# First expert layer with the hidden units on the partitions: w1 blocks as the stationary operand, 128 token slots moving

## The chip, the cores and the metric

The kernel runs on one core of one Trainium2 chip. The metric is the device time of a run in microseconds. The trace is one profiled run of the same program; its span is about 2 us shorter than the time. In the lines of the profile PE is TensorE, PEld its weight loads, PEldq the sequencer that feeds both, DVE is VectorE, ACT ScalarE, POOL GpSimd and SP SyncE. Runs over 1.5% above the fastest of the same kernel are called slow and are left out of comparisons.

## The reference, cut to what matters

The first half is a linear attention (8 batches, 8 heads, 576 positions). Its output `x` (4608 tokens of 512) goes through a mixture of 8 experts:

```python
h = np.maximum(x[b, s] @ w1[e], 0.0)          # 512 -> 1024
out[b, s] = p[e] * (h @ w2[e])                # 1024 -> 512
```

The expert `e` of a token is known only at run time: the argmax of a gate, or, behind a second gate, the expert of the token before.

## The kernel before

The kernel sorts tokens into pages of 128 slots, all of one expert. There are 38 pages here, in two epochs. The number `ev` (expert times the columns of one expert) is loaded into a TensorE register for each page, and every matmul that needs w1 or w2 addresses it through that register. Both weights lie complete in SBUF in bf16. This is the first layer of a page, with its transposes, and the second layer:

```python
def hidden(n, xt, ev_src, mid=lambda: None):
    ev = nc.values_load(ev_src, engines=(PE,), ...)
    h_ps = ps_p.tile([128, 8, 128], F32, name="pj").rearrange(...)
    for c in range(2):
        for dc in range(DC):                   # DC = 4
            nc.tensor.matmul(h_ps[:, c, :], lhsT=xt[:, dc, :],
                             rhs=w1_all[:, ds(ev + (dc * F + c * 512), 512)],
                             start=(dc == 0), stop=(dc == DC - 1))
        if c == 0:
            mid()                              # turns the next page's x
    h = arena[:, n % 3].rearrange("p (f c) -> p f c", c=128)
    nc.scalar.activation(h, h_ps..., Act.Relu)
    return h, ev

def hidden_t(h, n=FC):                         # FC = 8
    tp = ps_t.tile([128, FC, 128], BF, name="tp")
    for f in range(n):
        nc.tensor.transpose(tp[:, f], h[:, f], ident_bf)
    ...
    nc.vector.tensor_copy(ht[:, 0:n], tp[:, 0:n])
    if n < FC:                                 # the other half by DMA
        nc.sync.dma_start_transpose(out=ht[:, n:], in_=h[:, n:]...)

# output(), the second layer
for f in range(FC):
    nc.tensor.matmul(y_ps[:, 0, :], lhsT=htn[0][:, f],
                     rhs=w2_all[:, ds(ev + f * D, D)], ...)
```

Pages 0 to 16 are computed up to the relu while w2 is still being loaded. From page 17 on, first layers alternate with outputs, three outputs for two pages.

The softmax here doesn't subtract the row's maximum and nothing guards it: scores larger than these inputs give would overflow.

Of the kernel before, what the change touches and what calls it, by code (L numbers as in the profile page):

```python
# [23 lines left out]
NEP = 18  # L24
# [6 lines left out]
def kernel(  # L31
# [296 lines left out]
    rmask = consts.tile([128, 2, 9], F32)  # L328
    ids2 = consts.tile([128, 18, 2], BF)
    wt8 = consts.tile([128, E], F32)  # L330
    io128 = consts.tile([128, 128], BF)
    cpg = consts.tile([128, NC], F32)
# [8 lines left out]
    def gate_consts():  # L341
        wg3 = consts.tile([128, 2, 4, E + 1], BF)
        wgr = consts.tile([128, 4, E + 1], F32)
        nc.gpsimd.tensor_tensor(ident2, ident[:, 0:64], ident[:, 64:128], op=Alu.add)
        nc.gpsimd.iota(io128, pattern=[[1, 128]], base=0, channel_multiplier=0, **fdt)
        yield
# [5 lines left out]
        for a in range(2):  # L352
# [3 lines left out]
        yield  # L356
        nc.gpsimd.iota(ids2[:, :, 0].rearrange("p (a r) -> p a r", a=2), pattern=[[128, 2], [0, 9]], base=0,
                       channel_multiplier=1, **fdt)
        nc.gpsimd.iota(ids2[:, :, 1].rearrange("p (a r) -> p a r", a=2), pattern=[[0, 2], [1, 9]], base=1,
                       channel_multiplier=0, **fdt)  # L360
        nc.gpsimd.iota(wt8, pattern=[[-1, E]], base=E, channel_multiplier=0, **fdt)
        nc.gpsimd.iota(cpg, pattern=[[1, NC]], base=0, channel_multiplier=0, **fdt)
        yield
        nc.gpsimd.memset(onesb, 1.0)
# [16 lines left out]

    def gate(ep, gt, n):


# [71 lines left out]
        nc.vector.tensor_scalar(gpg, code, scalar1=7, scalar2=None, op0=Alu.logical_shift_right)  # L456
        slf, col = t18("slf"), t18("col")
        nc.vector.tensor_copy(slf, slot)
        if ep == 0:
            nc.vector.tensor_copy(col, gpg)  # L460
        else:
            nc.vector.tensor_scalar(col, gpg, scalar1=float(NEP), scalar2=over, op0=Alu.is_ge, op1=Alu.mult)
            nc.vector.tensor_tensor(col, col, gpg, op=Alu.add)
        if ep:
            yield
            yield

        oh, pg = t18("oh", 128, BF), t18("pg", NC, BF)
        ri = gt.tile([128, n, 2, NC], BF, name="ri")

        def parts(r_, v_, t_):
            shape = list(r_.shape)
            nc.vector.tensor_tensor(r_, pg[:, t_].unsqueeze(2).to_broadcast(shape), v_[:, t_].unsqueeze(3).to_broadcast(shape),
                                    op=Alu.mult)

        def build(g):
            t_ = slice(n * g, n * g + n)
            nc.vector.tensor_tensor(oh[:, t_], io128.unsqueeze(1).to_broadcast([128, n, 128]),
                                    slf[:, t_].to_broadcast([128, n, 128]), op=Alu.is_equal)
            nc.vector.tensor_tensor(pg[:, t_], cpg.unsqueeze(1).to_broadcast([128, n, NC]),  # L480
                                    col[:, t_].to_broadcast([128, n, NC]), op=Alu.is_equal)
            parts(ri, ids2, t_)

        build(0)
        yield
        l_ps = ps_k.tile([128, 2, NC], F32, name="kv")
        for g in range(18 // n):
            for i in range(n):
                nc.tensor.matmul(l_ps.rearrange("p a c -> p (a c)"), lhsT=oh[:, n * g + i],
                                 rhs=ri[:, i].rearrange("p a c -> p (a c)"),  # L490
                                 start=(g == 0 and i == 0), stop=(n * g + i == 17))
            yield
            if n * (g + 1) < 18:
                build(g + 1)
                yield
# [33 lines left out]
        nc.vector.tensor_scalar(over, gbs[:, E:E + 1], scalar1=float(-NEP), scalar2=over, op0=Alu.add, op1=Alu.add)  # L529
        lists[ep] = dict(idr=idr, ix=ix, lid=lid, tmp=(ex, fr, m_, rs, oh, pg, parts))  # L530

    def both(ep, n):
        yield from gate(ep, gt, n)
        yield from probs(ep, gt)

    def probs(ep, gt):

        ex, fr, m_, rs, oh, pg, parts = lists[ep].pop("tmp")

# [3 lines left out]

        v3, pr = t18("v3", 3, BF), t18("pr")
        rp = gt.tile([128, 6, 3, NC], BF, name="rp")
        nc.vector.tensor_reduce(rs, ex, axis=AX, op=Alu.add)
# [4 lines left out]
        for i in range(2):  # L551
            nc.vector.tensor_copy(v3[:, :, i:i + 1], pr)
            nc.vector.tensor_tensor(v3[:, :, 2:3] if i else pr, pr, v3[:, :, i:i + 1], op=Alu.subtract)
        if ep:
# [3 lines left out]
        for g in range(3):  # L558
            parts(rp, v3, slice(6 * g, 6 * g + 6))
            yield  # L560
            for i in range(6):
                nc.tensor.matmul(p_ps.rearrange("p a c -> p (a c)"), lhsT=oh[:, 6 * g + i],
                                 rhs=rp[:, i].rearrange("p a c -> p (a c)"),
                                 start=(g == 0 and i == 0), stop=(g == 2 and i == 5))
            yield
# [37 lines left out]
    WH = 17  # L603
    outs, hs, done, spare = [], {}, [], list(range(3, 9))
    NST = 2 * NEP + 2

    def hidden(n, xt, ev_src, mid=lambda: None):
        ev = nc.values_load(ev_src, engines=(PE,), min_val=0, max_val=(E - 1) * WE,
                            skip_runtime_bounds_check_because="multiples of the columns of one expert")
        h_ps = ps_p.tile([128, 8, 128], F32, name="pj").rearrange("p (a x) c -> p a (x c)", a=2)  # L610
        for c in range(2):
            for dc in range(DC):
                nc.tensor.matmul(h_ps[:, c, :], lhsT=xt[:, dc, :], rhs=w1_all[:, ds(ev + (dc * F + c * 512), 512)],  # L613
                                 start=(dc == 0), stop=(dc == DC - 1))
            if c == 0:
                mid()
        h = arena[:, n % 3].rearrange("p (f c) -> p f c", c=128)
        nc.scalar.activation(h, h_ps.rearrange("p a x -> p (a x)").rearrange("p (c f) -> p f c", f=FC), Act.Relu)  # L618
        return h, ev

    def hidden_t(h, n=FC):

        tp = ps_t.tile([128, FC, 128], BF, name="tp")
        for f in range(n):
            nc.tensor.transpose(tp[:, f], h[:, f], ident_bf)  # L625
        n_ = spare.pop(0) if spare else 0
        ht = arena[:, n_].rearrange("p (f c) -> p f c", c=128) if n_ else moh.tile([128, FC, 128], BF, name="ht")
        nc.vector.tensor_copy(ht[:, 0:n], tp[:, 0:n])  # L628
        if n < FC:
            nc.sync.dma_start_transpose(out=ht[:, n:], in_=h[:, n:].rearrange("p f c -> p (f c)"))  # L630
        return ht, n_

    def output(pg, htn, ev, last=False):
# [3 lines left out]
        for f in range(FC):  # L637
            nc.tensor.matmul(y_ps[:, 0, :], lhsT=htn[0][:, f], rhs=w2_all[:, ds(ev + f * D, D)],  # L638
                             start=(f == 0), stop=(f == FC - 1))
        if htn[1]:  # L640
            spare.append(htn[1])
# [23 lines left out]
    def page(j, nw, gates):  # L665
# [8 lines left out]

        if j < NST:
            hs[j] = hidden(j, xts.pop(j), pages[j][1], mid)
        gate_part()
        if j >= 1:
            h, ev = hs.pop(j - 1)
            done.append((pages[j - 1], hidden_t(h, FC // 2 if NEP <= j < NST - 1 else FC), ev))  # L680
        gate_part()
# [25 lines left out]
    for P in range(NP):  # L707
        for g, i, d_ in LK:
            t = max(9 * P + d_, i - 2) if g == 0 else 9 * P + d_
            at(t, cast_k, P, g, i, 0 <= t < LAG - 4)  # L710
        for r in range(9):
            at(9 * P + LAG - 4 + r // 2, cast_q, P, r)
        if P + 1 < NP:
            if P:
                at(9 * P - 5, load, P + 1, "k", 0)
            at(9 * P + 5, load, P + 1, "v", 0)
            at(9 * P - 1, load, P + 1, "k", 1)
            at(9 * P + 9, load, P + 1, "v", 1)
            at(9 * P + LAG + 1, load, P + 1, "q", 0)
# [22 lines left out]
    for t in range(NK + LAG + 3):  # L742
# [45 lines left out]
        if tk:  # L788
            for _ in range(t > 8 and t % 5 in (0, 2, 4)):
                w_load()  # L790
        else:
            for _ in range(3 if 0 not in lists else 0):
                w_load()
        if t == NK + 1:

            kctx.close()
            w2_all = pool("w2p", 1, side="right", **rw).tile([128, E * WE], BF)
            wdst[1] = w2_all
            gt = pool("gt", 1, side="right", **rw)
            ga = both(0, 6)  # L800
            next(ga)
# [10 lines left out]
    mo2 = pool("mo2", 4, **rw)  # L812
    moh = pool("moh", WH - 5, **rw)
    ga = both(1, 6)
    next(ga)
    for j in range(early[0], NST + 1):
        page(j, 3, True)
# [12 lines left out]
    def rest(i):  # L830
        with tc.If(nov > i):
            for d in range(2):
                pg = pages[2 * NEP + i + d]
                h, ev = hidden(d, turn(fetch(pg[0])), pg[1])
                output(pg, hidden_t(h), ev)
            if i + 2 < NOV:
# [33 lines left out]
```

## Time and profile before

The median of three runs is 333.03 us (332.88 to 334.21), the profiled span 330.9 us.

| stretch of the span | what runs | PE busy of it | what sets its length |
|---|---|---|---|
| 0 to 126 us | attention | 70% (48 to 86% by 20 us) | mixed |
| 126 to 155 us | first routing | 11.7 of 29.0 us | a chain on DVE, DMA |
| 155 to 213.5 us | first layer of pages 0 to 16, second routing, w2 load | 49.9 of 58.5 us | mostly PE |
| 213.5 to 321 us | first layer of pages 17 to 37, all outputs | all of it | PE |

The prediction shows the lines.

### The profile page before, as it was taken

The numbers are of one execution on the slowest core, as the hardware profiler recorded it, in microseconds if no ns is written. First come the engines' busy times: TensorE is split into PE (matmuls) and PEld (weight loads), VectorE is DVE, ScalarE is ACT, GpSimd is POOL, SyncE is SP. The second block draws the span as 40 slices with busy tenths as digits, with TensorE's granted clock in tenths as the row PEclk, the third lists the DMA queues.
The fourth block names the chain that finished last, engine by engine and source line by source line (L and its number), as shares of the span: only waits on it lengthen the run. The fifth ranks groups of instructions, "written<-read, shape, count | busy, mean of one in ns | idle before, by whom it ended". The sixth has DMA issues, their size and how long they took to land. (4 is left out here: it accounts for less than half of the span.)

```text
span 330.9 us, 7843 instructions
## 1 busy us (share of the span) xinstructions
PE 257.2 (78%) x2789; PEld 151.7 (46%) x2809; DVE 183.2 (55%) x406; ACT 154.1 (47%) x230; POOL 195.8 (59%) x299
## 2 busy tenths in 40 slices
PE   2585488768787775722998885999999999999980
PEld 1464256546464553411565453554444444444430
DVE  2677188788879768980354776423333333323440
ACT  1586498888889865510555452532122221222000
POOL 3677787698498595356377653325555657432550
PEclk9859779999899959555799997999999999999996
DMA  7999989999888789999689996338668666532330
GB/s 230 391 411 408 315 238 326 368 271 301 285 239 259 239 150 202 224 223 222 130 167 206 226 226 164 81 82 184 171 173 176 189 148 171 168 112 79 129 133 32
DMA packets 52649, 69.89 MB, mean 211 GB/s; under 512 B 25552, under 2 KB 27088, under 8 KB 52608
## 3 DMA queue, kind: packets, MB, share of 16 engines
q0 software_dynamic: 14176, 31.14, 42.4%
q1 hardware_dynamic: 34352, 33.43, 30.9%
q10 hardware_dynamic: 4080, 4.77, 4.2%
q8 instruction: 26, 0.43, 0.5%
q14 instruction: 15, 0.12, 0.1%
HBM read 67.16 MB, written 14.68 MB: 247 GB/s over the span
## 5 line engine op out<-in xcount | busy, mean ns | idle before, releaser
L613 PE MATMUL pj<-w_all,xt 128*128 x291 | 75.2, 389 | 2.6 <-ACT xt L599 1.4
L618 ACT ACTIVATE arena<-pj 128x1024 bf16<-128x1024 f32 x38 | 38.9, 1023 | 75.3 <-PE pj L613 70.9
L644 POOL DMA_INDIRECT out_dram<-y,idr x38 | 37.8, 995 | 51.3 <-DVE y L643 47.3
L584 POOL DMA_INDIRECT xg<-x_tok,ix x36 | 37.4, 1038 | 27.3 <-PE tp L597 16.5
L212 DVE TENSOR_REDUCE kmx<-pj 128x8 f32<-128x1024 f32 x36 | 44.0, 1222 | 16.1 <-ACT kvb L251 8.4
L232 POOL TENSOR_TENSOR va<-vs,ek 128x512 bf16<-128x512 f32 (+1 forms) x40 | 38.2, 958 | 21.0 <-ACT ek L221 15.3
L156 POOL DMA_DIRECT2D w_all<-in_moe_w_dram x64 | 35.8, 565 | 16.4 <-DMA w_all<-in_moe_w_dram 15.3
L281 ACT ACTIVATE qp<-pj 128x1024 bf16<-128x1024 f32 x36 | 37.5, 1043 | 12.4 <-PE pj L275 12.3
L613 PEld LDWEIGHTS <-xt 128*128 128x128 bf16 x304 | 29.0, 99 | 30.2 <-issue 2.2
L218 ACT ACTIVATE kp<-pj 128x1024 bf16<-128x1024 f32 x36 | 37.3, 1037 | 11.2 <-DVE kmx L212 11.2
L643 DVE TENSOR_SCALAR y<-po,prb 128x512 f32<-128x512 f32 x24 | 18.0, 751 | 29.0 <-PE po L638 29.0
L183 PE MATMUL tp<-ident_bf,kb 128*128 128x128 bf16 x144 | 17.1, 246 | 17.1 <-POOL kb L110 8.1
L206 PE MATMUL pj<-om_bd,kt 128*128 128x256 bf16 x144 | 25.8, 310 | 2.9 <-ACT qp L281 1.8
L305 DVE TENSOR_TENSOR xr<-po,rd 128x512 bf16<-128x512 f32 x36 | 24.9, 692 | 1.2
L599 ACT COPY xt<-tp 128x512 bf16<-128x512 bf16 x18 | 10.5, 584 | 30.2 <-PE tp L597 29.1
L638 PE MATMUL po<-w_all,ht 128*128 x103 | 24.5, 379 | 0.1
L628 DVE COPY ht<-tp 128x1024 bf16<-128x1024 bf16 (+1 forms) x20 | 11.9, 597 | 22.5 <-PE tp L625 22.5
L116 POOL CAST qb<-arena 128x512 bf16<-128x512 f32 x36 | 21.1, 612 | 3.9 <-DMA arena<-in_q_dram 3.9
L729 ACT COPY qt<-tp 128x512 bf16<-128x512 bf16 x36 | 21.6, 601 | 3.6 <-DVE kt L727 2.7
L638 PEld LDWEIGHTS <-ht 128*128 128x128 bf16 x160 | 15.1, 98 | 16.1
L628 DVE COPY arena<-tp 128x512 bf16<-128x512 bf16 (+1 forms) x18 | 9.2, 514 | 22.0 <-PE tp L625 22.0
L727 DVE COPY kt<-tp 128x512 bf16<-128x512 bf16 x36 | 15.0, 417 | 11.3 <-PE tp L183 11.2
(152 smaller groups left out, 394.7 us busy)
## 6 DMA issues: line engine op xcount, KB each, us to landing
w_all<-in_moe_w_dram POOLq DMA_DIRECT2D x64, 256.0 KB, 7.9
vs<-in_v_dram SPq DMA_DIRECT2D x8, 1152.0 KB, 12.5
arena<-in_q_dram SPq DMA_DIRECT2D x4, 2304.0 KB, 15.1
ks<-in_k_dram SPq DMA_DIRECT2D x7, 1152.0 KB, 13.8
x_tok<-xr ACTq DMA_DIRECT2D x16, 256.0 KB, 5.7
ks<-in_k_dram SPq DMA_DIRECT2D x1, 640.0 KB, 5.6
out_dram<-y,idr POOLq DMA_INDIRECT x38, 2.9
xg<-x_tok,ix POOLq DMA_INDIRECT x36, 3.7
```

The source lines that it names most:

```text
L156: nc.gpsimd.dma_start(out=wdst[l][:, ds(e * WE + i * 1024, 1024)].rearrange("p (c f) -> p c f", f=w), in_=src[e].rearrange(("(c p) f -> p ...
L206: nc.tensor.matmul(pj[:, 2 * i:2 * i + 2, :].rearrange("p a d -> p (a d)"), lhsT=kts[t][:, i], rhs=om_bd, start=True, stop=True)
L212: nc.vector.tensor_reduce(mx, kpj[t], axis=AX, op=Alu.max)
L218: nc.scalar.activation(kp, kpj.pop(t), Act.Exp, scale=scale)
L232: nc.gpsimd.tensor_tensor(va[:, x, 0:Dh].rearrange("p (r h) d -> p r h d", h=4), vv, ek[:, x].rearrange("p (r h) o -> p r h o", h=4).to_br ...
L281: nc.scalar.activation(qp, qpj.pop(s), Act.Exp, scale=scale)
L305: nc.vector.tensor_tensor(xrs[s][:, u % 2, :].rearrange("p (g h d) -> p g h d", g=2, h=4), ov[:, :, :, 0:Dh], rd.to_broadcast([128, 2, 4, ...
L584: nc.gpsimd.indirect_dma_start(out=xg, out_offset=None, in_=src, in_offset=bass.IndirectOffsetOnAxis(ap=ix, axis=0), bounds_check=TE - 1, ...
L613: nc.tensor.matmul(h_ps[:, c, :], lhsT=xt[:, dc, :], rhs=w1_all[:, ds(ev + (dc * F + c * 512), 512)], start=(dc == 0), stop=(dc == DC - 1))
L618: nc.scalar.activation(h, h_ps.rearrange("p a x -> p (a x)").rearrange("p (c f) -> p f c", f=FC), Act.Relu)
L638: nc.tensor.matmul(y_ps[:, 0, :], lhsT=htn[0][:, f], rhs=w2_all[:, ds(ev + f * D, D)], start=(f == 0), stop=(f == FC - 1))
L644: s_ = nc.gpsimd.indirect_dma_start(out=out_flat, out_offset=bass.IndirectOffsetOnAxis(ap=idr[:, c:c + 1], axis=0), in_=y, in_offset=None, ...
```

## The change

A matmul has a stationary operand (`lhsT`, which a weight load fetches first) and a moving one (`rhs`). The new first layer makes 128 columns of w1 stationary and streams the 128 slots. The result comes out with units on the partitions, as the second layer wants its stationary operand, so neither transposes nor their copies are needed. Block `f` takes every eighth column, because w2 is stored with unit 8p+f on partition p.

```diff
-    def hidden(n, xt, ev_src, mid=lambda: None):
+    def hidden(xt, ev_src, mid=lambda: None):
...
-        for c in range(2):
+        h_ps = ps_p.tile([128, FC, 128], F32, name="pj")
+        for f in range(FC):
             for dc in range(DC):
-                nc.tensor.matmul(h_ps[:, c, :], lhsT=xt[:, dc, :], rhs=w1_all[:, ds(ev + (dc * F + c * 512), 512)],
-                                 start=(dc == 0), stop=(dc == DC - 1))
+                nc.tensor.matmul(h_ps[:, f], lhsT=w1_all[:, ds(ev + (dc * F + f), 128, step=FC)],
+                                 rhs=xt[:, dc, :], start=(dc == 0), stop=(dc == DC - 1))
...
-    def hidden_t(h, n=FC):
...
```

The rest of the diff re-tunes what stands around it. The one-hot tiles of the routing get a layout with step 1 in all operands, all in bf16. Two instead of three weight loads are issued per step after the attention. All 9 places of `arena` hold relu outputs, some routing steps come later, and one cast of k comes a step earlier.

More of the change, by code (lines that the diff above doesn't have):

```diff
@@ L328 @@
     rmask = consts.tile([128, 2, 9], F32)
-    ids2 = consts.tile([128, 18, 2], BF)
+    ids2 = consts.tile([128, 2, 18], BF)
     wt8 = consts.tile([128, E], F32)
-    io128 = consts.tile([128, 128], BF)
+    io6 = consts.tile([128, 128, 6], BF)
+    cpg6 = consts.tile([128, NC, 6], BF)
     cpg = consts.tile([128, NC], F32)
@@ L344, in gate_consts @@
         nc.gpsimd.tensor_tensor(ident2, ident[:, 0:64], ident[:, 64:128], op=Alu.add)
-        nc.gpsimd.iota(io128, pattern=[[1, 128]], base=0, channel_multiplier=0, **fdt)
+        nc.gpsimd.iota(io6, pattern=[[1, 128], [0, 6]], base=0, channel_multiplier=0, **fdt)
         yield
@@ L356, in gate_consts @@
         yield
-        nc.gpsimd.iota(ids2[:, :, 0].rearrange("p (a r) -> p a r", a=2), pattern=[[128, 2], [0, 9]], base=0,
+        nc.gpsimd.iota(ids2[:, 0].rearrange("p (a r) -> p a r", a=2), pattern=[[128, 2], [0, 9]], base=0,
                        channel_multiplier=1, **fdt)
-        nc.gpsimd.iota(ids2[:, :, 1].rearrange("p (a r) -> p a r", a=2), pattern=[[0, 2], [1, 9]], base=1,
+        nc.gpsimd.iota(ids2[:, 1].rearrange("p (a r) -> p a r", a=2), pattern=[[0, 2], [1, 9]], base=1,
                        channel_multiplier=0, **fdt)
@@ L362, in gate_consts @@
         nc.gpsimd.iota(cpg, pattern=[[1, NC]], base=0, channel_multiplier=0, **fdt)
+        nc.gpsimd.iota(cpg6, pattern=[[1, NC], [0, 6]], base=0, channel_multiplier=0, **fdt)
         yield
@@ L380, with gate @@
     lists = {}
-    def gate(ep, gt, n):
+    def gate(ep, gt):
         lg = lgs[ep]
@@ L456, in gate @@
         nc.vector.tensor_scalar(gpg, code, scalar1=7, scalar2=None, op0=Alu.logical_shift_right)
-        slf, col = t18("slf"), t18("col")
-        nc.vector.tensor_copy(slf, slot)
+        slf, col = gt.tile([128, 18], BF, name="slf"), gt.tile([128, 18], BF, name="col")
+        nc.vector.tensor_copy(slf.unsqueeze(2), slot)
         if ep == 0:
-            nc.vector.tensor_copy(col, gpg)
+            nc.vector.tensor_copy(col.unsqueeze(2), gpg)
         else:
-            nc.vector.tensor_scalar(col, gpg, scalar1=float(NEP), scalar2=over, op0=Alu.is_ge, op1=Alu.mult)
-            nc.vector.tensor_tensor(col, col, gpg, op=Alu.add)
+            cof = t18("cof")
+            nc.vector.tensor_scalar(cof, gpg, scalar1=float(NEP), scalar2=over, op0=Alu.is_ge, op1=Alu.mult)
+            nc.vector.tensor_tensor(col.unsqueeze(2), cof, gpg, op=Alu.add)
         if ep:
@@ L466, in gate, with parts @@
             yield
-        oh, pg = t18("oh", 128, BF), t18("pg", NC, BF)
-        ri = gt.tile([128, n, 2, NC], BF, name="ri")
-        def parts(r_, v_, t_):
+        oh = gt.tile([128, 3, 128, 6], BF, name="oh")
+        pg = gt.tile([128, 3, NC, 6], BF, name="pg")
+        rp = gt.tile([128, 3, NC, 6], BF, name="rp")
+        ri = rp[:, 0:2]
+        def parts(r_, v_, g):
             shape = list(r_.shape)
-            nc.vector.tensor_tensor(r_, pg[:, t_].unsqueeze(2).to_broadcast(shape), v_[:, t_].unsqueeze(3).to_broadcast(shape),
-                                    op=Alu.mult)
+            nc.vector.tensor_tensor(r_, pg[:, g].unsqueeze(1).to_broadcast(shape),
+                                    v_[:, :, 6 * g:6 * g + 6].unsqueeze(2).to_broadcast(shape), op=Alu.mult)
         def build(g):
-            t_ = slice(n * g, n * g + n)
-            nc.vector.tensor_tensor(oh[:, t_], io128.unsqueeze(1).to_broadcast([128, n, 128]),
-                                    slf[:, t_].to_broadcast([128, n, 128]), op=Alu.is_equal)
-            nc.vector.tensor_tensor(pg[:, t_], cpg.unsqueeze(1).to_broadcast([128, n, NC]),
-                                    col[:, t_].to_broadcast([128, n, NC]), op=Alu.is_equal)
-            parts(ri, ids2, t_)
+            for o_, c_, x_ in ((oh, io6, slf), (pg, cpg6, col)):
+                nc.vector.tensor_tensor(o_[:, g], c_, x_[:, 6 * g:6 * g + 6].unsqueeze(1).to_broadcast(list(c_.shape)),
+                                        op=Alu.is_equal)
+            parts(ri, ids2, g)
         build(0)
@@ L486, in gate @@
         l_ps = ps_k.tile([128, 2, NC], F32, name="kv")
-        for g in range(18 // n):
-            for i in range(n):
-                nc.tensor.matmul(l_ps.rearrange("p a c -> p (a c)"), lhsT=oh[:, n * g + i],
-                                 rhs=ri[:, i].rearrange("p a c -> p (a c)"),
-                                 start=(g == 0 and i == 0), stop=(n * g + i == 17))
+        for g in range(3):
+            for i in range(6):
+                nc.tensor.matmul(l_ps.rearrange("p a c -> p (a c)"), lhsT=oh[:, g, :, i],
+                                 rhs=ri[:, :, :, i].rearrange("p a c -> p (a c)"),
+                                 start=(g == 0 and i == 0), stop=(g == 2 and i == 5))
             yield
-            if n * (g + 1) < 18:
+            if g < 2:
                 build(g + 1)
@@ L529, in gate, with both @@
         nc.vector.tensor_scalar(over, gbs[:, E:E + 1], scalar1=float(-NEP), scalar2=over, op0=Alu.add, op1=Alu.add)
-        lists[ep] = dict(idr=idr, ix=ix, lid=lid, tmp=(ex, fr, m_, rs, oh, pg, parts))
-    def both(ep, n):
-        yield from gate(ep, gt, n)
+        lists[ep] = dict(idr=idr, ix=ix, lid=lid, tmp=(ex, fr, m_, rs, oh, rp, parts))
+    def both(ep):
+        yield from gate(ep, gt)
+        if ep:
+            yield
+            yield
         yield from probs(ep, gt)
     def probs(ep, gt):
-        ex, fr, m_, rs, oh, pg, parts = lists[ep].pop("tmp")
+        ex, fr, m_, rs, oh, rp, parts = lists[ep].pop("tmp")
         def t18(nm, w=1, dt=F32):
             return gt.tile([128, 18, w], dt, name=nm)
-        v3, pr = t18("v3", 3, BF), t18("pr")
-        rp = gt.tile([128, 6, 3, NC], BF, name="rp")
+        v3, pr = gt.tile([128, 3, 18], BF, name="v3"), t18("pr")
         nc.vector.tensor_reduce(rs, ex, axis=AX, op=Alu.add)
@@ L551, in probs @@
         for i in range(2):
-            nc.vector.tensor_copy(v3[:, :, i:i + 1], pr)
-            nc.vector.tensor_tensor(v3[:, :, 2:3] if i else pr, pr, v3[:, :, i:i + 1], op=Alu.subtract)
+            nc.vector.tensor_copy(v3[:, i].unsqueeze(2), pr)
+            nc.vector.tensor_tensor(v3[:, 2].unsqueeze(2) if i else pr, pr, v3[:, i].unsqueeze(2), op=Alu.subtract)
         if ep:
@@ L558, in probs @@
         for g in range(3):
-            parts(rp, v3, slice(6 * g, 6 * g + 6))
+            parts(rp, v3, g)
             yield
             for i in range(6):
-                nc.tensor.matmul(p_ps.rearrange("p a c -> p (a c)"), lhsT=oh[:, 6 * g + i],
-                                 rhs=rp[:, i].rearrange("p a c -> p (a c)"),
+                nc.tensor.matmul(p_ps.rearrange("p a c -> p (a c)"), lhsT=oh[:, g, :, i],
+                                 rhs=rp[:, :, :, i].rearrange("p a c -> p (a c)"),
                                  start=(g == 0 and i == 0), stop=(g == 2 and i == 5))
@@ L603 @@
     WH = 17
-    outs, hs, done, spare = [], {}, [], list(range(3, 9))
+    outs, done, spare = [], [], list(range(9))
     NST = 2 * NEP + 2
-    def hidden(n, xt, ev_src, mid=lambda: None):
+    def hidden(xt, ev_src, mid=lambda: None):
         ev = nc.values_load(ev_src, engines=(PE,), min_val=0, max_val=(E - 1) * WE,
                             skip_runtime_bounds_check_because="multiples of the columns of one expert")
-        h_ps = ps_p.tile([128, 8, 128], F32, name="pj").rearrange("p (a x) c -> p a (x c)", a=2)
-        for c in range(2):
+        h_ps = ps_p.tile([128, FC, 128], F32, name="pj")
+        for f in range(FC):
             for dc in range(DC):
-                nc.tensor.matmul(h_ps[:, c, :], lhsT=xt[:, dc, :], rhs=w1_all[:, ds(ev + (dc * F + c * 512), 512)],
-                                 start=(dc == 0), stop=(dc == DC - 1))
-            if c == 0:
+                nc.tensor.matmul(h_ps[:, f], lhsT=w1_all[:, ds(ev + (dc * F + f), 128, step=FC)],
+                                 rhs=xt[:, dc, :], start=(dc == 0), stop=(dc == DC - 1))
+            if f == 3:
                 mid()
-        h = arena[:, n % 3].rearrange("p (f c) -> p f c", c=128)
-        nc.scalar.activation(h, h_ps.rearrange("p a x -> p (a x)").rearrange("p (c f) -> p f c", f=FC), Act.Relu)
-        return h, ev
-    def hidden_t(h, n=FC):
-        tp = ps_t.tile([128, FC, 128], BF, name="tp")
-        for f in range(n):
-            nc.tensor.transpose(tp[:, f], h[:, f], ident_bf)
-        n_ = spare.pop(0) if spare else 0
-        ht = arena[:, n_].rearrange("p (f c) -> p f c", c=128) if n_ else moh.tile([128, FC, 128], BF, name="ht")
-        nc.vector.tensor_copy(ht[:, 0:n], tp[:, 0:n])
-        if n < FC:
-            nc.sync.dma_start_transpose(out=ht[:, n:], in_=h[:, n:].rearrange("p f c -> p (f c)"))
-        return ht, n_
+        n_ = spare.pop(0) if spare else None
+        ht = (moh.tile([128, FC, 128], BF, name="ht") if n_ is None
+              else arena[:, n_].rearrange("p (f c) -> p f c", c=128))
+        nc.scalar.activation(ht, h_ps, Act.Relu)
+        return (ht, n_), ev
     def output(pg, htn, ev, last=False):
@@ L639, in output @@
                              start=(f == 0), stop=(f == FC - 1))
-        if htn[1]:
+        if htn[1] is not None:
             spare.append(htn[1])
@@ L673, in gate_part @@
                 next(ga, None)
-        if j < NST:
-            hs[j] = hidden(j, xts.pop(j), pages[j][1], mid)
+        done.append((pages[j],) + hidden(xts.pop(j), pages[j][1], mid))
         gate_part()
-        if j >= 1:
-            h, ev = hs.pop(j - 1)
-            done.append((pages[j - 1], hidden_t(h, FC // 2 if NEP <= j < NST - 1 else FC), ev))
         gate_part()
@@ L708 @@
         for g, i, d_ in LK:
-            t = max(9 * P + d_, i - 2) if g == 0 else 9 * P + d_
+            t = max(9 * P + d_, i - 2) if g == 0 else 9 * P + d_ - (P > 0 and i == 1)
             at(t, cast_k, P, g, i, 0 <= t < LAG - 4)
@@ L791 @@
         else:
-            for _ in range(3 if 0 not in lists else 0):
+            for _ in range(2 if 0 not in lists else 0):
                 w_load()
@@ L799 @@
             gt = pool("gt", 1, side="right", **rw)
-            ga = both(0, 6)
+            ga = both(0)
             next(ga)
@@ L812 @@
     mo2 = pool("mo2", 4, **rw)
-    moh = pool("moh", WH - 5, **rw)
-    ga = both(1, 6)
+    moh = pool("moh", WH - 8, **rw)
+    ga = both(1)
     next(ga)
-    for j in range(early[0], NST + 1):
+    for j in range(early[0], NST):
         page(j, 3, True)
@@ L833, in rest @@
                 pg = pages[2 * NEP + i + d]
-                h, ev = hidden(d, turn(fetch(pg[0])), pg[1])
-                output(pg, hidden_t(h), ev)
+                ht, ev = hidden(turn(fetch(pg[0])), pg[1])
+                output(pg, ht, ev)
             if i + 2 < NOV:
```

## The prediction

> **What bounds the kernel now.** I read the page's 40 slices first, then busy time by stretch, then the group table, then single lines of the program in short windows.
>
> The stretches (window, length, busy us with counts of PE, PEld, DVE, ACT, POOL, then PE clock, DMA share, GB/s) divide the run:
>
> ```profile
> 126.00:155.00 29.00, 11.66 (x175) 7.48 (x173) 20.62 (x66) 9.44 (x13) 13.58 (x21) 0.63 1.09 228
> 155.00:213.50 58.50, 49.94 (x443) 29.75 (x452) 32.85 (x97) 27.75 (x37) 32.57 (x43) 0.92 0.84 172
> 222.40:295.10 72.70, 72.28 (x378) 34.81 (x385) 25.29 (x44) 16.44 (x17) 40.20 (x40) 1.00 0.68 169
> 295.10:321.00 25.90, 25.75 (x134) 12.23 (x134) 10.72 (x15) 2.08 (x3) 11.21 (x12) 1.00 0.31 113
> ```
>
> Up to 126 us it is attention. 126 to 155 is routing: DVE carries a chain, PE is nearly idle, the DMA queues are full. From 155 to 213.5 the first layer of pages 0 to 16 runs, mixed with the tail of attention, the second routing and the w2 load. From 213.5 to 321, pages 17 to 37 run their first layer and all 38 pages their second; PE is never idle at clock 1.00. So PE sets the second stage outright and most of the first. What PE does there:
>
> ```profile
> L613 PE MATMUL pj<-w_all,xt x291: 375/379/635, 155.9 to 302.7; 128*128 x146
> L625 PE MATMUL tp<-ident_bf,arena 128*128 128x128 bf16 x228 | 19.0, 219 | 0.1
> L628 DVE COPY ht<-tp 128x1024 bf16<-128x1024 bf16 (+1 forms) x20 | 11.9, 597 | 22.5 <-PE tp L625 22.5
> ```
>
> L613 is the first layer (8 matmuls of 512 columns a page, 304 in all, 13 records missing), L625 the transposes to be removed, L628 half of their evacuations. The means of one (379, 219 ns) are pipelined latencies, not costs. In the trace's records consecutive 512-column matmuls start 216 ns apart and consecutive transposes 55 to 56 ns apart.
>
> This accounts for the second stage: from 222.4 to 295.1 us there are 16 pages of first layer and 24 of second. 16 x (8 x 0.216 + 4 transposes x 0.056) + 24 x 8 x 0.216 = 31.2 + 41.5 = 72.7 us, exactly the stretch. It is array time and nothing else.
>
> The lines I rest on most are ones the page does not count as busy. PEldq is the sequencer that feeds PE; each query here covers one line of the program in one window:
>
> ```profile
> L613 PEldq FUSED_REGOPS  x304: 42/46/51, 155.8 to 299.4; - x152
> L638 PEldq FUSED_REGOPS  x304: 42/46/46, 217.0 to 318.7; - x152
> L613 PEldq FUSED_REGOPS  x8: 42/46/46, 241.3 to 242.2; - x8
> L638 PEldq FUSED_REGOPS  x8: 42/46/46, 242.4 to 243.3; - x8
> L608 PEldq TENSOR_LOAD <-ei x38: 296/303/592, 155.2 to 298.0; - x38
> ```
>
> Every matmul whose weights are chosen by the expert register `ev` has a register instruction of its own: 304 for 38 pages x 8, in each layer. They execute in the sequencer. In a run of sixteen they start at 241.3 to 243.3 us, about 0.13 us apart; over the raw records of 155 to 325 us the commonest spacing, and the floor, is 0.124 us (346 of 600 gaps are 122 to 126 ns). So register instruction + weight load + matmul costs the sequencer 0.124 us however short the matmul is. At 512 columns (0.216 us of array) that is hidden. The once-a-page load of `ev` costs more: from the last register instruction before it to the first after is about 0.66 us in the second stage, 0.53 beyond the usual spacing. These instructions also stand behind waits: at 171.02 us the transposes L597 get their buffer, and the next register instruction starts at 171.03, some 0.6 us after the one before.
>
> **What the Trainium skill says.** "TensorE: Matmul & The Clock Gate", section "Wait — 56ns, not 53.3ns?", gives 55.6 and 215.7 ns between warm matmuls of 128 and 512 columns; the trace agrees (55 to 56, 216). "Perfetto Trace Analysis", "Sequencer Loop": engine instructions are pushed into a queue, control instructions execute in the sequencer itself; that is what the register instructions show. "Advanced Engine Details and Errata", "SBUF Cachelines": cachelines have 16 bytes, and a different line per access is penalised. The new weight blocks step 8 bf16 = 16 bytes, a line for each element; no run so far has a strided weight load, so its cost is open. "VectorE: DVE Perf Modes", "The perf-mode tier table": tensor_tensor reaches 2x in bf16. The old one-hot build (768 elements in 0.95 us) shows no such gain; the new one has step 1 in all operands.
>
> **The change part by part.**
>
> Removed: 304 matmuls of 512 columns, 228 relu transposes, 38 DVE copies out of PSUM (0.43 or 0.69 us), 19 DMA transposes. Array time removed: 38 x 1.73 + 228 x 0.056 = 78.5 us. The copies lie beside PE, except around 198 to 202.5 us, where a page waits some 4 us for a copy queued behind routing work on DVE.
>
> Added: 38 x 32 = 1216 matmuls of 128 columns, with 1216 dynamic, strided weight loads. Array time, if strided loads hide like the present ones: 1216 x 0.056 = 68.1 us. By array time alone the change gains 10 us, plus the stall of 4. I take this to be its intent.
>
> Sequencer time is another matter. Each of the 32 blocks has its own offset from `ev` (dc*F + f), so I expect 32 register instructions a page instead of 8: 32 x 0.124 = 3.97, plus 0.53 for the load, 4.50 us a page. The array needs only 1.8. The sequencer becomes the bound of the first layer.
>
> Second stage: 21 pages x 4.50 = 94.5; 31 outputs fed between them at 8 x 0.124 = 0.99 give 30.8; the last 7 outputs have no first layer beside them and stay at array pace, 7 x 1.73 = 12.1. Sum 137.4 us against 107.5 now: +30.
>
> First stage: 17 x (4.50 + 4 x 0.056 for the x transposes) = 80.3, and about 110 other short pairs at about 0.05 = 5.5: 86 against 58.5 now, +27. The DVE stall saved is in this already.
>
> Routing: six builds of (0.950 + 0.352 + 0.558) and six of 0.752 us of DVE. At half cost the first routing saves some 2.6 + 1.0 us on the path to the first page. Two instead of three weight loads a step should let the gathered rows land sooner: now PE waits 7.4 us for them at 154 us. Together I take -5; the parts of the second routing are not on a DVE path any more.
>
> Sum: 333 + 30 + 27 - 5 = 385 us.
>
> **Rivals.**
> (a) The array stays the bound and the gain of about 10 to 14 us arrives: 319 to 325. For it: every schedule detail of the diff (9 spare buffers, later yields, fewer weight loads) has been retuned around the change, and if several addresses were computed in one instruction the 0.124 would not multiply. Against it: 304 register instructions for 304 matmuls on both lines now, and a sharp floor of 0.124 us.
> (b) Strided weight loads are slow. Present ones read 98 ns but sustain 56 ns. Up to 124 ns a load hides under the sequencer. At 0.2 us it would bind: 32 x 0.2 = 6.4 + 0.5 us a page, some 75 us more than in my sum. I give it one in eight.
> (c) The first stage stays bound by the w2 load: DMA share is near 1.1 up to 200 us. The loads end at about 205 us, though, and the stage under my count at 236, so this moves little.
> (d) The sequencer runs ahead during outputs and hides part. A total bounds this: the sequencer's 30-odd us of outputs are already counted at 0.99, not 1.73. Nothing more can be hidden.
>
> **Range and chances.** Inside the main theory the uncertain terms are the static pairs and waits (5 us either way), routing (4) and the load of `ev` (6): 370 to 400. The rivals widen both sides; (a) and partial versions of it pull the low end. 80% range 357 to 408. Faster by over 2%: 0.08; within 2%: 0.04; slower: 0.88.
>
> **What would show it.** Right: 1216 register instructions on the first-layer line at a floor near 0.124 us; first-layer matmuls starting 0.12 us apart, not 0.056; a page each 4.5 to 5 us in the first stage; sixteen pages of the second stage taking about 96 instead of 72.7 us; PE idle time put down to "issue"; PE clock perhaps dropping. Wrong: one register instruction for several matmuls, or starts 56 ns apart (rival a); starts about 0.2 us apart (rival b); the one-hot build still at 0.95 us (routing term).

## The result, and the profile after

The changed kernel takes 487.72 us (median of 4 runs, 486.55 to 488.82) against 332.95 us for the kernel before on the same chip. The ratio is 1.464, 95% interval 1.458 to 1.470. Ratios here and below are the mean time of one kernel's fast runs over that of the other's in the same rounds, so not quite the ratio of the medians quoted. The direction was predicted; 488 lies far outside 357 to 408.

Two rows of the page of the changed kernel, each digit one fortieth of 484.8 us in tenths:

```profile
PE   4666768777758999999999999999999999999992
PEclk9599997997855555555555577889888779888797
```

PE looks full from 150 us on, and yet its granted clock is 0.5 for the first layers. The busy figure counts latencies of matmuls that hardly overlap any more. Two stretches, with the columns of the prediction's first fence: pages 3 to 15, then pages 20 to 36.

```profile
170.20:266.50 96.30, 93.26 (x531) 67.56 (x531) 16.13 (x67) 21.12 (x27) 29.00 (x41) 0.50 0.59 103
300.40:450.70 150.30, 148.03 (x753) 89.38 (x752) 20.00 (x30) 17.23 (x17) 41.44 (x41) 0.87 0.23 68
```

A page of the first stage takes 96.3 / 13 = 7.41 us, one of the second, with its 1.5 outputs, 150.3 / 17 = 8.84 us. The kernel before needed 72.7 / 16 = 4.54 us for the latter. DVE, ACT and the DMA queues are far from full. The sequencer's lines of the changed kernel, whole run first, then one window of 2 us (in all of them: count, duration min/median/max in ns, first and last start in us):

```profile
L618 PEldq FUSED_REGOPS  x2432: 37/46/51, 143.3 to 457.9; - x188
L633 PEldq FUSED_REGOPS  x304: 42/46/46, 281.5 to 472.8; - x152
L613 PEldq TENSOR_LOAD <-ei x38: 295/302/494, 142.7 to 450.7; - x38
L618 PEldq FUSED_REGOPS  x20: 46/46/46, 304.0 to 306.0; - x20
L618 PEld LDWEIGHTS <-w_all x10: 141/143/149, 304.0 to 305.9; 128*128 x10
L618 PE MATMUL pj<-xt,w_all x11: 215/216/217, 303.9 to 306.0; 128*128 128x128 bf16 x11
```

The first line holds the answer. The first layer has 2432 register instructions, not 1216: two for each of the 1216 blocks. In the window, 20 of them start in 2.0 us, about 0.105 us apart, with 10 weight loads and 11 matmuls among them. In the raw records 931 of the 1216 blocks start in the order register instruction, weight load, register instruction, matmul (in the others register instructions have run ahead); from 160 us on, 2124 of the 2621 gaps between register instructions of both layers lie between 100 and 115 ns. A block therefore costs 2 x 0.104 = 0.208 us, and matmuls of 128 columns follow each other at that distance (the median of their spacing is 208 ns). Why two: the list of built instructions shows that the matmul also carries the register address of its stationary operand, although a separate weight load has fetched it, so the same address is worked out once for each of the two.

This pace gives nearly the whole time. A page is 64 x 0.104 = 6.66 us plus the load of `ev`, against 7.41 measured. In the second stage 1.5 outputs of 0.99 us come on top. Beyond what was predicted a page costs 64 x 0.104 - 32 x 0.124 = 2.69 us; 38 x 2.69 = 102 us; 385 + 102 = 487. That it fits to the microsecond is luck: page 0 loads its `ev` 12.5 us earlier than in the kernel before, where 5 were counted, and the stretch from page 17's load of `ev` (273.9 us) to the last matmul takes 201 us, where the corrected sum has 137 + 21 x 2.69 = 194.

The routing term can be read from one line of each kernel, the one-hot build before and after:

```profile
L478 DVE TENSOR_TENSOR oh<-io,slf x6: 947/949/959, 130.5 to 192.9; 128x768 bf16<-128x768 bf16 x6
```

```profile
L482 DVE TENSOR_TENSOR oh<-io,slf x6: 546/551/605, 127.8 to 223.3; 128x768 bf16<-128x768 bf16 x6
```

0.95 us became 0.55, and the first page's `ev` is loaded at 142.7 instead of 155.2 us. That part works; it is drowned.

### The profile page after: what moved, and what is told of

It reads as the page before. It is cut to its first block, busy times and chain, and to the rows that moved or that the text cites. A ratio compares the mean times of both kernels' runs of the same rounds, so it can differ in the third digit from the quotient of the medians.

```text
span 484.8 us, 11274 instructions
## 1 busy us (share of the span) xinstructions
PE 422.2 (87%) x3493; PEld 279.0 (58%) x3493; DVE 157.1 (32%) x368; ACT 153.7 (32%) x230; POOL 198.6 (41%) x300
## 3 DMA queue, kind: packets, MB, share of 16 engines
q0 software_dynamic: 14176, 31.14, 29.7%
## 5 line engine op out<-in xcount | busy, mean ns | idle before, releaser
L618 PE MATMUL pj<-xt,w_all 128*128 128x128 bf16 x1216 | 228.0, 247 | 8.8 <-issue 2.3
L618 PEld LDWEIGHTS <-w_all 128*128 x1216 | 160.3, 145 | 76.7 <-issue 10.6
L625 ACT ACTIVATE arena<-pj 128x1024 bf16<-128x1024 f32 x26 | 26.6, 1023 | 155.1 <-PE pj L618 155.1
L633 PE MATMUL po<-w_all,arena 128*128 x128 | 41.7, 485 | 0.2 <-issue 0.2
L633 PEld LDWEIGHTS <-arena 128*128 128x128 bf16 x208 | 22.8, 110 | 29.8 <-issue 13.9
L625 ACT ACTIVATE ht<-pj 128x1024 bf16<-128x1024 f32 x12 | 12.3, 1023 | 48.6 <-PE pj L618 48.6
L183 PEld LDWEIGHTS <-kb 128*128 128x128 bf16 x144 | 11.4, 108 | 20.1 <-issue 8.1
L633 PE MATMUL po<-w_all,ht 128*128 x64 | 22.7, 520 | 0.0
```

Of the source, the lines that this page charges most:

```text
L183: nc.tensor.transpose(tp[:, w, i], source(t, nm, i).rearrange("p h d -> p (h d)"), ident_bf)
L618: nc.tensor.matmul(h_ps[:, f], lhsT=w1_all[:, ds(ev + (dc * F + f), 128, step=FC)], rhs=xt[:, dc, :], start=(dc == 0), stop=(dc == DC - 1))
L625: nc.scalar.activation(ht, h_ps, Act.Relu)
L633: nc.tensor.matmul(y_ps[:, 0, :], lhsT=htn[0][:, f], rhs=w2_all[:, ds(ev + f * D, D)], start=(f == 0), stop=(f == FC - 1))
```

## The experiments

Theory 1: the sequencer is the bound, through two register instructions a block. Rival theory 2: strided weight loads are slow in the array. Rival theory 3: the low clock is a cause, not a consequence. The second register instruction was never removed alone.

**Constant addresses, blocks still strided.** Outputs are wrong.

```diff
-  lhsT=w1_all[:, ds(ev + (dc * F + f), 128, step=FC)],
+  lhsT=w1_all[:, ds(dc * F + f, 128, step=FC)],
```

> The changed kernel, but every first-layer block is taken at a constant address (always expert 0, so the outputs are wrong on purpose). The weight blocks keep their step of 8 elements. Theory 1 (the sequencer is the bound: two register instructions of 0.104 us for each of 32 blocks): with no register instruction left on the first-layer line a page costs the array 32 x 0.061 = 1.95 us, the second stage goes back to about 73 us for 16 pages and 24 outputs, the time falls to 312 to 335 us, and the PE clock comes back to about 0.9. Theory 2 (strided weight loads are slow in the array): they are still strided, so the time stays above 440 us. Theory 3 (the granted clock of 0.5 is a cause of its own, set by the mix of instructions): the clock stays near 0.5 in the first stage and the time above 400 us.

Measured: 324.77 us, ratio to the kernel before 0.971 (0.964 to 0.979). The lines of the first layer, and the 17 pages of the second stage that answer to the second stretch above:

```profile
L618 PEld LDWEIGHTS <-w_all x1216: 142/146/170, 145.7 to 297.8; 128*128 128x128 bf16 x174
L618 PE MATMUL pj<-xt,w_all x1216: 217/225/314, 146.7 to 297.9; 128*128 128x128 bf16 x174
216.90:294.20 77.30, 77.30 (x748) 54.05 (x746) 20.01 (x30) 16.57 (x17) 41.66 (x42) 1.00 0.53 136
```

No register instruction is left on this line, the same strided loads are there at about the same latency (146 ns; 144 in the changed kernel), and 17 pages take 77.3 instead of 150.3 us at clock 1.00. Theories 2 and 3 fall: the strided loads stayed and the time did not; the clock came back with the work. What the low clock itself can have cost is little: in the changed kernel's second stretch the register instructions and loads of `ev` alone make about 17 x (64 x 0.104 + 0.40 + 1.5 x 0.99) = 145 of the 150.3 us (0.40 is what a load of `ev` adds to the spacing there), an estimate that leaves 5 us for all else. And the run with 128 moving columns, below, loses its time at clock 1.00.

**Contiguous blocks through the register.**

```diff
-  lhsT=w1_all[:, ds(ev + (dc * F + f), 128, step=FC)],
+  lhsT=w1_all[:, ds(ev + (dc * F + f * 128), 128)],
...
-  src[e].rearrange(("(c p) f -> p c f", "(p c) f -> p c f")[l], p=128)
+  src[e].rearrange(("(c p) f -> p c f", "(c p) f -> p c f")[l], p=128)
```

> The changed kernel with contiguous weight blocks (unit f*128+c in block f; w2 is loaded in the order that fits, so the outputs stay right), still addressed through the expert register. Theory 1: 64 register instructions a page as before, so 478 to 492 us, within 2% of the changed kernel. Theory 2: no strided load is left, so the time falls to the predicted 385 us or below. Theory 3 as theory 1.

Measured: 491.29 us, ratio 1.471 (1.457 to 1.484), the changed kernel's 1.464 within the interval. The weight loads became shorter (102 instead of 144 ns), the register instructions stayed:

```profile
L618 PEldq FUSED_REGOPS  x2432: 37/46/51, 143.9 to 458.5; - x188
L618 PEld LDWEIGHTS <-w_all x1216: 95/102/152, 144.3 to 458.5; 128*128 x174
```

Taking the stride away alone gains nothing.

**Constant addresses and contiguous blocks.** Both edits together, outputs wrong.

> Both together: constant addresses and contiguous blocks (outputs wrong on purpose). It differs from the static strided run only in the step of the weight blocks. Theory 1: consecutive matmuls start 56 instead of 61 ns apart, 1216 x 0.005 = 6 us at most, so 0 to 2.5% faster than the static strided run. Theory 2: far faster than the static strided run, by 100 us or more.

Measured: 322.94 us, ratio 0.965 (0.958 to 0.973).

```profile
L618 PEld LDWEIGHTS <-w_all x1216: 95/98/152, 147.1 to 294.0; 128*128 128x128 bf16 x174
216.60:290.60 74.00, 74.00 (x748) 50.16 (x747) 20.00 (x30) 16.38 (x16) 41.60 (x42) 1.00 0.60 141
```

The stride is worth 77.3 - 74.0 = 3.3 us on 17 pages of 32 blocks, 6 ns a block: weight loads read 146 instead of 98 ns, but matmuls start 61 to 62 instead of 56 ns apart. On the whole run the two intervals overlap; 2.9 us of the gain are lost at the very end, where the new order of w2 has a cost of its own (see the last experiment). The stride is a small cost that the sequencer hid in the changed kernel.

**One register instruction a block.** The kernel before, with w1 still moving, in pieces of 128 columns; outputs right.

```diff
             for dc in range(DC):
-                nc.tensor.matmul(h_ps[:, c, :], lhsT=xt[:, dc, :], rhs=w1_all[:, ds(ev + (dc * F + c * 512), 512)], ...)
+                for b_ in range(4):
+                    nc.tensor.matmul(h_ps[:, c, b_ * 128:b_ * 128 + 128], lhsT=xt[:, dc, :],
+                                     rhs=w1_all[:, ds(ev + (dc * F + c * 512 + b_ * 128), 128)],
+                                     start=(dc == 0 and b_ == 0), stop=(dc == DC - 1), ...)
```

> The kernel before, with its first layer cut into 32 matmuls of 128 moving columns instead of 8 of 512: xt stays stationary at a constant address, so there is one register instruction a block and no strided weight load; transposes and all else as before; outputs right. This is the cost that the prediction assumed. Theory 1: 0.124 us a block, a page 32 x 0.124 + 0.5 = 4.5 us, so 375 to 395 us. If a register instruction costs nothing that counts (theory 2 or 3 alone), the array needs 32 x 0.056 = 1.8 us as 8 x 0.216 did, and the time stays at 330 to 340 us.

Measured: 394.88 us, ratio 1.182 (1.172 to 1.193), at the upper edge of what was expected. One page of it:

```profile
L614 PEldq FUSED_REGOPS  x32: 42/46/46, 230.1 to 234.2; - x32
L614 PEld LDWEIGHTS <-xt x32: 95/96/98, 230.3 to 234.2; 128*128 128x128 bf16 x32
L614 PE MATMUL pj<-w_all,xt x32: 216/216/219, 230.3 to 234.3; 128*128 x32
```

32 register instructions start from 230.1 to 234.2 us, 0.13 us apart; in the raw records of both layers from 160 us on, 1213 of 1495 gaps are 122 to 126 ns. This is the price the prediction had worked out, paid in a kernel that streams the same columns as before, at clock 1.00 from 180 to 330 us. It costs 61 us here (394.88 against 334.33 on the same chip); the changed kernel has two register instructions a block and pays 0.208 instead of 0.124 us.

**Half of the blocks at constant addresses.** Every second `f`, outputs wrong.

```diff
-  lhsT=w1_all[:, ds(ev + (dc * F + f), 128, step=FC)],
+  lhsT=w1_all[:, ds((ev if f % 2 == 0 else 0) + (dc * F + f), 128, step=FC)],
```

> The changed kernel with every second block (f odd) at a constant address: 32 register instructions a page instead of 64, all loads still strided, outputs wrong on purpose. Theory 1: a page costs the sequencer 16 x 0.208 + 16 x about 0.05 + 0.7 = 4.8 instead of 7.4 us, the time falls by about 38 x 2.5 = 95 us to 380 to 405 us: half the register instructions, a good half of the loss. Strided loads or a clock of its own: no change, about 487 us.

Measured: 364.48 us, one run, state unknown; the kernel before on that chip had 337.4 us.

```profile
L618 PEldq FUSED_REGOPS  x394: 42/46/51, 170.0 to 220.0; - x197
220.00:340.00 120.00, 118.19 (x934) 83.55 (x949) 23.75 (x38) 23.09 (x23) 46.71 (x47) 1.00 0.35 98
```

The gain of 123 us on the changed kernel (on another chip, so good to some 4 us) is above the 82 to 107 us that the expected times stand for. 38 x 32 register instructions less at 0.104 us make 126 us, so the blocks with constant addresses cost the sequencer next to nothing, where I had put 0.05 us each. The trace agrees: across four such blocks the median gap between register instructions is 129 instead of 104 ns, some 6 ns a block. So the loss goes with the number of register instructions, and the strided loads, all still there, matter little. The clock is 1.00.

**The rest of the change alone.** The old first layer with its transposes in the changed kernel (`hidden`, `hidden_t`, their calls and the 12 + 6 relu buffers of before); outputs right.

> The changed kernel with the old first layer put back (8 matmuls of 512 columns with w1 moving, relu outputs transposed); the new routing build, the w2 load pacing and the later steps of the second routing stay; outputs right. Theory 1 says that the whole loss is in the first layer's register instructions, so the rest of the change is neutral or a small gain: the DVE builds of the routing at half cost and first pages some 5 us earlier give 322 to 333 us. Rival: part of the loss comes from the rest (fewer weight loads a step, later routing steps), then 340 us or more.

Measured: 333.08 us (median of 6) against 337.40, ratio of fast runs 0.985 (0.981 to 0.989). Two of the six runs were slow, the profiled one among them, so its trace isn't compared. The median lies at the upper edge of the 322 to 333 us expected; the ratio, applied to the 333 us of the first chip, gives 328. The rest of the change is a gain of 1.5%, 5 us; none of the loss comes from it.

**A version with the weights staged.** Pages 0 to 16 as in the run above. From page 17 on, DVE copies the expert's block of w1 to a constant place, in halves, a page ahead:

```diff
+    def stage(ev_src, h_):
+        evd = nc.values_load(ev_src, engines=(DVE,), ...)
+        wst = wsp.tile([128, DC, 512], BF, name="wst")
+        nc.vector.tensor_copy(wst, w1_all[:, ds(evd, WE)].rearrange("p (d a x) -> p d a x", a=2, x=512)[:, :, h_])
...
+        for f in range(FC):
+            for dc in range(DC):
+                nc.tensor.matmul(h_ps[:, f], lhsT=wsts[j, f // 4][:, dc, (f % 4) * 128:(f % 4) * 128 + 128],
+                                 rhs=xt[:, dc, :], ...)
```

> A try at a version that beats both: the kernel of the run with the rest only for pages 0 to 16; from page 17 on DVE copies the expert's first-layer block in two halves to a constant place (one register instruction and one load of the register a copy), and the first layer is computed as in the change, units on the partitions, with contiguous blocks at constant addresses; no relu transposes there; outputs right. Theory 1: a page of the second stage then costs the array 32 x 0.056 = 1.8 us instead of 8 x 0.216 + 4 x 0.056 = 1.95, so two pages and three outputs take 8.8 instead of 9.1 us; 21 pages give 3 us against the run with the rest only: 318 to 330 us. Rival: the copies come late, because each stands in DVE's queue behind the outputs' evacuations, and PE waits a microsecond or more a page: 335 to 360 us.

Measured: 334.24 us against 337.40, ratio 0.990 (0.987 to 0.994); outputs right. The 334 us lie above the 318 to 330 expected; with the ratio applied to the 333 us of the first chip they would be 330. There is no gain over the rest alone. One late output in the order of time:

```profile
308.34 1.89 PE L667 MATMUL pj<-w_all,arena 128*128 x8
308.62 0.98 POOL L673 DMA_INDIRECT out_dram<-y,idr  x1 [1.14 <-DVE y L672]
309.80 0.75 DVE L672 TENSOR_SCALAR y<-po,prb 128x512 f32<-128x512 f32 x1 [1.45 <-DMA out_dram<-y,idr]
310.60 1.67 PE L667 MATMUL po<-w_all,arena 128*128 x7 [0.37 <-DVE y L672]
```

The copies work: the last matmul starts at 313.8 us, in the kernel before at 320.9. But I had paid for the two staged tiles by halving the output buffers to two. DVE's evacuation waits 1.45 us for the DMA scatter of an earlier output, and PE in turn waits for DVE. Such waits come to 8.6 us in seven outputs. The profiled run also lost about 4 us once near 275 us: a staging copy waits 4.46 us for an event that the profile doesn't name, and PE then 2.7 us for the copy.

**The staged version with its buffers back.**

```diff
-    WH = 17
+    WH = 16
-    mo2 = pool("mo2", 2, **rw)
+    mo2 = pool("mo2", 4, **rw)
-    moh = pool("moh", 10, **rw)
+    moh = pool("moh", 8, **rw)
```

> The staged version with the four output buffers of the kernel before (the first try had two, and its last seven outputs waited 1 to 1.5 us each for the scatter before), paid for by switching to the staged form and to outputs one page earlier (page 16) with two fewer relu buffers; outputs right. In the first try the array's two-page stretches took 8.75 us as worked out and the last matmul ended 7 us before that of the kernel before, but the tail gave most of it back. If that reading is right, the time falls by 3 to 6 us against the first try, to a ratio of 0.965 to 0.985 to the kernel before; if the copies themselves cost the gain, it stays at 0.99.

Measured: 328.96 us (median of 6) against 335.11, ratio 0.984 (0.979 to 0.988); outputs right. The same place in the tail:

```profile
307.77 1.89 PE L667 MATMUL pj<-w_all,arena 128*128 x8
307.97 0.75 DVE L672 TENSOR_SCALAR y<-po,prb 128x512 f32<-128x512 f32 x1 [0.98 <-PE po L667]
309.00 0.98 POOL L673 DMA_INDIRECT out_dram<-y,idr  x1 [0.75 <-DVE y L672]
```

DVE waits for PE again, as it should. The ratio lies at the upper edge of the 0.965 to 0.985 expected. Both kernels are beaten, the one before by 1.6%; by the rule of 2% that is "unclear", since the interval reaches from 1.2 to 2.1%. Against the rest alone (0.985 on another chip) nothing can be told: the intervals cover each other. Two pages and three outputs take 8.6 to 8.8 us in most of the second stage, against 8.9 to 9.2 in the kernel before; over its ten such pairs that is some 3 us, what the page-by-page sum gave. The last matmul starts at 312.7 us, 8 us earlier than before, but the span ends only 5 us earlier. The difference is in POOL's closing instructions, first the kernel before, then this one:

```profile
L865 POOLq DRAIN  x3: 50/103/3010, 327.0 to 330.6; - x3
L906 POOLq DRAIN  x3: 50/103/5297, 319.6 to 325.5; - x3
```

The longest drain takes 5.30 instead of 3.01 us, and the semaphore instruction before it 1.47 instead of 0.91, together 2.9 us. The four kernels that load w2 in the order for contiguous blocks all show this, the six others none of it; their queue q0, which carries the weights, moves 18272 instead of 14176 packets. So the cost goes with the loading order, not with the staging; the order was never changed alone.

## Why the prediction was wrong, point by point

- **What bounds the kernel now: right.** The array sets the second stage, to the tenth of a microsecond in the sum, and constant addresses left that stage array-bound (74.0 to 77.3 us for 17 pages).
- **The sequencer becomes the bound of the first layer: right.** It is the mechanism of the whole loss; removing the register instructions takes all of it away.
- **"I expect 32 register instructions a page instead of 8": this is the step that failed.** There are 64, and a page of the first stage takes 7.41 us, not 4.5 to 5. I carried over the count of one per matmul from a form in which the register addresses the moving operand. With the stationary operand addressed through the register, the weight load and the matmul each get one. The profile of before could not show it, since no weight load there used a register.
- **0.124 us a block: right for what it assumed**, as the run with 128 moving columns shows (394.88 us; the sum without its routing term, which that run doesn't have, is 390). It is the commonest spacing but not quite "the floor": from 160 us on, 40 of the 599 gaps in the kernel before are 120 ns and one is 103. For the new form the term is 2 x 0.104 = 0.208. With it, 385 becomes 487.
- **The term of 0.05 us for short pairs with constant addresses: too large.** The run with half of the blocks at constant addresses shows some 6 ns a block.
- **Routing, -5 us: right in size, partly by luck.** The rest alone measured 1.5%, about 5 us. The build fell from 0.95 to 0.55 us, a little less than by half. But in the changed kernel the first page comes 12.5 us earlier, more than was counted; what else brings it forward was not separated.
- **Rival (a), the array's gain of 10 to 14 us: wrong for the kernel as written.** With constant addresses it is there (medians 10 and 11 us below those of the kernel before, ratios 0.971 and 0.965), about 5 us of it from the rest of the change.
- **Rival (b), slow strided loads: wrong.** 6 ns a block. It had the larger time, and it would have been tempting to take the result for its proof: by its own terms it stands 38 x (6.4 + 0.5 - 4.50) = 91 us above my sum, not the 75 written there, which gives 476; and the starts 0.208 us apart even match its "about 0.2 us". Only the counts of register instructions, and the runs that separated stride from register, tell them apart.
- **The range** was widened downward for rival (a) and hardly upward. The count of register instructions, the factor of the largest term, had been given no uncertainty at all.

## What to carry to other kernels

In this kernel an address from a register had a price per instruction in the sequencer that feeds the engine (0.104 to 0.124 us), not in the array, and the busy figures did not show it: count the register instructions on the line, take the spacing of their starts, and compare with the array time of what they feed. Put the run-time operand on the side with few, long instructions (8 matmuls of 512 columns hide it, 32 of 128 do not), and never assume that the count stays the same when the register moves to the other operand. Where many short matmuls must use run-time weights, a copy to a constant place needs one register instruction and can be done by an engine with time to spare (0.69 us on DVE for half a page's block here); in this kernel that only undid the loss and gained some 3 us in the second stage.

## What the Trainium skill lacked or had wrong

- No page has the cost of a register address on TensorE. The runs show 0.124 us for register instruction, weight load and matmul with the register on the moving operand, and 2 x 0.104 us with it on the stationary operand. It belongs to "Perfetto Trace Analysis", "Sequencer Loop", which says of control instructions only that they start executing in the sequencer's microcode.
- "TensorE: Matmul & The Clock Gate", "Back-to-back issue gap", gives about 81 ns sustained for pairs of weight load and matmul at 128 columns and 131 ns at 512. Here contiguous pairs of 128 columns sustain 56 ns (the run with constant addresses and contiguous blocks), and pairs of 512 columns 216 ns (the kernel before). The 55.6 and 215.7 ns that the page gives without weight loads fit pairs as well.
- "Advanced Engine Details and Errata", "SBUF Cachelines", states a penalty for a new line at each access without a size for weight loads. With a step of 16 bytes it was 146 instead of 98 ns in latency, but only 62 instead of 56 ns between matmuls.
- "TensorE: Matmul & The Clock Gate" ties the clock to how busy PE is, without saying what counts as busy. In the changed kernel one matmul of 128 columns each 0.208 us was granted 0.50 for 96 us on end; with one each 0.124 us (128 moving columns) or with half of the blocks at constant addresses the grant was 1.00.
